# Routing the first two batches in one block and starting the experts at step 13 instead of step 15

## The chip, the core and the metric

The kernel runs on one core of a Trainium2 chip. The metric is the device time of one execution in microseconds (us). The engines of the core work side by side, each through its own instruction queue in order: TensorE (PE, matrix products), VectorE (DVE), ScalarE (ACT), GpSimd (POOL), and SyncE (SP), which here only issues transfers. A transfer issued by POOL with a list of row numbers (an indirect DMA) scatters rows to places in memory.

## The reference, cut to what matters

The input is `x`, 8 batches of 2496 x 256. A two-dimensional Fourier transform is taken of each batch and its real part gives 19968 tokens of 256 features. Each token goes to one of 8 experts (two matrices with a ReLU between them), and its result is scaled by two gate values.

```python
X = np.fft.fft(np.fft.fft(x, axis=1), axis=2).real      # (8, 2496, 256) -> 19968 tokens
logits = X @ w_gate
e_idx = np.argmax(logits, axis=1)
gate_w = softmax(logits)[arange, e_idx]
eom = sigmoid(X @ w_output_gate)
for e in range(8):
    mask = e_idx == e
    out[mask] = gate_w[mask, None] * eom[mask, e, None] * (relu(X[mask] @ w1[e]) @ w2[e])
```

## The kernel before

**Fourier part.** A batch is cut into five chunks along the sequence; chunk m (0 to 39) belongs to batch m // 5. A chunk is loaded (`load_x`, L302), folded by `fold1` (L413, L416, L417, mostly on POOL; L416 and L417 exist from batch 3 on, `LB`) and `fold2` (L429 to L443, mostly DVE), its energy is summed on ACT (L451), and `dstage` (L482 to L486, PE) with `devac` (L494 on ACT, L495 on DVE) transforms the features. Then come five steps of a batch: step n belongs to batch b = n // 5 and has the place i = n % 5. Each is one `sstage` (L521, PE) with `sevac` (L536 to L556, DVE and ACT), which leaves rows of tokens in on-chip memory. During the steps of batch b the loop `steps()` also folds chunks of the next batch or two (`AHEAD` says up to which chunk, place by place), takes the next batch's energy (at place 1) and runs its `dstage` (places 2 to 4).

**Routing.** `gating(b)` starts at the first step of batch b + 1. It finds each token's expert and its row in the scratch memory `scr` (L564 to L647, DVE and ACT, with two small matmuls L597 and L598), and issues 20 scatters (L653, POOL) that write the rows. It is a generator in phases: a `yield "C"` ends a phase, and the loop lets it go on one phase per step. After scatters 4, 9 and 14 (`SPL`) it stops too, so the 20 scatters are spread over four steps with folds of later chunks between them on POOL's queue.

**Tables and experts.** `table_a(i)` lists blocks of tokens for the experts; the first table (`NAS[0]` = 12 slots of 256 tokens) covers the batches 0 and 1 (`BAS`). It ends with `slot_scales` (L712 to L717), which needs the weight scales `wsc`. Those come from the energies of all 16 weight matrices: each is loaded whole (`wload`, L363, two buffers `wt`) and squared on ACT (`wsquare`, L367), at a pace set in `steps()`, and `wscales` (L371 to L378) ends it. A slot of the experts loads its tokens transposed (`load_x_`, L1075, and their gate values L1076), has its weights loaded (`load_w`, L1089) and split into two 16-bit parts (`conv`, L1095 on ACT and L1096 on DVE), runs `mm1` (L1115) and `mm2` (L1135), and scatters the result (L1143, POOL).

**What sets the order.** Up to the end of the routing the queues of SP and POOL follow the order of the program text (`PH1`); the order on PE, ACT and DVE is worked out at build time by a simulated schedule and is then fixed. Steps 0 to `FSTART` = 15 are run before the experts begin. After that `background()` hands out the remaining steps between pieces of the expert slots, at rates worked out from `work`. `load_x` keeps five chunk buffers in the pool `px` and two more in `pw`, the pool on the right side that also holds `wt`; when `pw` is closed, its space goes to the experts' pool `fr` (raw weights, split weights, tokens).

Of the kernel before, what the change touches and what calls it, by code (L numbers as in the profile page):

```python
# [17 lines left out]
NB, S, D, E, F = 8, 2496, 256, 8, 1024  # L18
# [47 lines left out]
FSTART = 5 * BA + MARGIN  # L66

W0, NW = 2, 2

AHEAD = (5, 6, 7, 8, 9), (4, 5, 6, 7, 8)  # L70
# [160 lines left out]
def fft_moe_kernel(ctx: ExitStack, tc: tile.TileContext, xl, wg, w1, w2, tde, tdo, gt, ts0, tsm, tsr, tsq, cst, tid, out):  # L231
# [44 lines left out]
    if True:  # L276
# [16 lines left out]
        def load_x(n=NB * KC):  # L293

            while n and len(xq) < NB * KC:
                q = pw if held[pw] < NX2 and len(xq) < FSTART + 8 else px
                if held[q] == (NX2 if q is pw else NX):
                    break
                held[q] += 1
                b, c = divmod(len(xq), KC)  # L300
                t = q.tile([128, 8, HN], F32, name="xt", tag="xt", bufs=NX2 if q is pw else NX)
                nc.sync.dma_start(t, xl[b, c])  # L302
                xts[b, c] = t
                xq.append(q)
                n -= 1
# [75 lines left out]
        gens = []  # L381

# [36 lines left out]
        def fold2(b, c):  # L419
# [24 lines left out]
            for k in done:  # L444
                xts.pop((b, k))
                held[xq[b * KC + k]] -= 1
                load_x()
                if b == 0:
                    continue
                sq = pf.tile([128, 4, 128], mybir.dt.bfloat16, name="sq", tag="sq", bufs=1)  # L450
                nc.scalar.activation(sq[:, :, 0:KW[k]], f[k].rearrange("p a b n -> p (a b) n")[:, :, 0:KW[k]], AF.Square,  # L451
                                     scale=1.0 if h else 1.5, accum_out=st[b]["en"][:, k:k + 1])
# [105 lines left out]
        def gating(b):  # L558
# [98 lines left out]
            for j in range(20):  # L657
                if b < NB - 1:
                    scatter(j)
                    if j in SPL:  # L660
                        yield "C"
                else:
                    deferred.append(lambda j=j: scatter(j))
# [66 lines left out]
        def table_a(i):  # L730
# [54 lines left out]
            yield  # L785
            yield from slot_scales(ea, n, i)
# [145 lines left out]
        def start():  # L932
# [19 lines left out]
            for c in range(KC):  # L952
                if c > 1:
                    dstage(0, c)
                devac(0, c)

        def steps():
            wk = 0
            fc = KC
            for n in range(5 * NB):  # L960
                b, i = divmod(n, 5)
                if i == 0 and b > 0:
                    add_gen(gating(b - 1))
                smalls.clear()
                ds_ = ((), (), (0, 1), (2, 3), (4,))[i] if b + 1 < NB else ()
# [8 lines left out]
                while fc <= min(KC * (b + 1) + AHEAD[b >= BA][i], KC + 3 * n + 2):  # L974
# [14 lines left out]
                if i == 1 and b + 1 < NB:  # L989
                    energy(b + 1)  # L990
                    energy_sum(b + 1)
                    scale(b + 1)
                weave(piece("A"))
                while wk <= 2 * E and wk < (n - W0 + 1) * (2 * E + 1) / (FSTART - W0):
# [6 lines left out]
                if n == W0 - 1:  # L1001
                    for k in range(NW):
                        wload(k)
# [11 lines left out]
    if True:  # L1015
# [132 lines left out]
        def experts():  # L1148
            chained(load_x_, 0)
# [3 lines left out]
            chained(load_x_, 1)  # L1153
            for h in range(2):
                conv(0, 0, h)
            yield "i"
# [73 lines left out]
    with tc.manual_schedule(engines=PH1):  # L1230
        start()
        steps_ = steps()
        for m in steps_:
            if m == ("step", FSTART):
                break
        rp.close()
        fx.append(pl(ctx, name="fr", bufs=2, side="right"))
# [6 lines left out]
        for _ in table_a(0):  # L1244
            pass
        add_raw(fx[0])
        add_wbuf(fx[0])
# [3 lines left out]
        work = [5 * (b - a) + 45 * C_TAB for a, b in zip(BAS, BAS[1:])] + [5 * (NB - BAS[-1]) - MARGIN + 28 * C_SCAT + 50 * C_TAB + 3.5]  # L1251
        rates = [w / (9.0 * (e - s_)) for w, s_, e in zip(work, [0] + ends, ends)]
        acc, slot = 0.0, 0
        fg = experts()
# [39 lines left out]
```

## Time and profile before

| What | us |
| --- | --- |
| median of 3 runs | 1174.66 |
| lowest and highest of them | 1174.36 and 2767.52 |
| the profiled execution, its own time | 1159.36 |
| its span, first to last instruction | 1157.5 |
| VectorE busy | 833.0 (72%) |
| ScalarE busy | 731.6 (63%) |
| GpSimd busy | 498.6 (43%) |

A row of a timeline gives start, duration, engine, line, operation, the tiles written and read, the number of instructions and, in brackets, how long the engine was idle before it and what ended that. A row of stretches gives a window, its length, the busy time of each engine with its instructions in brackets, the clock granted to TensorE as a share of full speed, the share of time that the DMA engines were busy, and GB/s. A row of waits gives who waited for whom: us in total, times, longest. A row of groups gives busy us, mean ns of one, and idle time before them.

### The profile page before, as it was taken

The numbers are of one execution on the slowest core, as the hardware profiler recorded it, in microseconds if no ns is written. First come the engines' busy times: TensorE is split into PE (matmuls) and PEld (weight loads), VectorE is DVE, ScalarE is ACT, GpSimd is POOL, SyncE is SP. The second block draws the span as 40 slices with busy tenths as digits, with TensorE's granted clock in tenths as the row PEclk, the third lists the DMA queues.
The fourth block names the chain that finished last, engine by engine and source line by source line (L and its number), as shares of the span: only waits on it lengthen the run. The fifth ranks groups of instructions, "written<-read, shape, count | busy, mean of one in ns | idle before, by whom it ended". The sixth has DMA issues, their size and how long they took to land.

```text
span 1157.5 us, 28573 instructions
## 1 busy us (share of the span) xinstructions
PE 1052.7 (91%) x10060; PEld 934.4 (81%) x10060; DVE 833.0 (72%) x1535; ACT 731.6 (63%) x1216; POOL 498.6 (43%) x430
## 2 busy tenths in 40 slices
PE   3877469989999999998999999999999989999998
PEld 3666458878788887887878888889989979998887
DVE  7876797878988747568445454588777867787684
ACT  2598657666666654553445454587777767777684
POOL 5418873786577444462564122223222322322231
PEclk9998779999999999999999999999999999999999
DMA  7778554755547545464767524557457464655651
GB/s 285 300 260 346 214 161 137 222 164 149 168 144 183 138 131 151 137 166 143 186 182 177 142 57 122 154 159 196 128 170 201 125 166 113 175 166 147 183 130 30
DMA packets 158213, 194.09 MB, mean 168 GB/s; under 512 B 117885, under 2 KB 118527, under 8 KB 156020
## 3 DMA queue, kind: packets, MB, share of 16 engines
q1 hardware_dynamic: 142100, 149.68, 46.6%
q0 software_dynamic: 15824, 42.14, 10.9%
q8 instruction: 79, 1.29, 0.5%
q14 instruction: 66, 0.54, 0.2%
q10 hardware_dynamic: 144, 0.44, 0.1%
HBM read 193.47 MB, written 43.46 MB: 205 GB/s over the span
## 4 chain that ended last, share of the span: by engine, by line
PE 63%; DVE 11%; issue 8%; POOL 6%; ACT 5%; DMA 3%; SPq 2%; another core or an unknown queue 0%; POOLq 0%; DVEq 0%; ACTq 0%
PE hp L1115 30%; PE yp L1135 29%; PE psb_t L521 3%; POOL scr L653 2%; POOL out_dram L1143 2%; DVE w1b L1096 1%; DVE rt L549 1%; DMA raw1b<-in_w_dram 1%; DVE hl L1120 1%; POOL xt L413 1%; SPq L1057 1%; ACT wt L367 1%; DVE w0b L1096 1%; DVE xt L432 1%; ACT w1b L1095 1%
## 5 line engine op out<-in xcount | busy, mean ns | idle before, releaser
L1115 PE MATMUL hp<-xr,w0b 128*128 128x256 f16 (+2 forms) x4224 | 482.8, 264 | 20.9 <-DVE hl L1120 13.7
L1135 PE MATMUL yp<-w1b,hh 128*128 128x256 f16 x2608 | 450.4, 273 | 6.7 <-issue 3.6
L1143 POOL DMA_INDIRECT out_dram<-y,xf x163 | 214.7, 1317 | 554.1 <-ACT y L1142 520.2
L1115 PEld LDWEIGHTS <-w0b 128*128 128x128 f16 x4224 | 384.6, 98 | 70.4 <-issue 15.4
L1135 PE MATMUL yp<-w1b,hl 128*128 128x256 f16 (+3 forms) x1304 | 356.0, 273 | 2.0 <-issue 2.0
L1135 PEld LDWEIGHTS <-hh 128*128 128x128 f16 x2608 | 251.9, 98 | 40.3 <-issue 11.9
L1119 ACT ACTIVATE hh<-hp 128x512 f16<-128x512 f32 (+4 forms) x352 | 194.0, 554 | 131.6 <-PE hp L1115 112.9
L1120 DVE SCALAR_TENSOR_TENSOR hl<-hp,hh 128x512 f16<-128x512 f32 (+4 forms) x352 | 222.0, 637 | 68.2 <-ACT hh L1119 56.9
L1096 DVE SCALAR_TENSOR_TENSOR w1b<-raw1b,ssc,w1b 128x1024 f16<-128x1024 f32 x144 | 186.3, 1294 | 111.7 <-ACT w1b L1095 90.3
L1096 DVE SCALAR_TENSOR_TENSOR w0b<-raw0b,ssc,w0b 128x1024 f16<-128x1024 f32 x144 | 190.2, 1324 | 69.6 <-ACT w0b L1095 51.7
L653 POOL DMA_INDIRECT scr<-rows,desti x160 | 178.6, 1116 | 73.3 <-issue 43.8
L1095 ACT ACTIVATE w0b<-raw0b,ssc 128x1024 f16<-128x1024 f32 x144 | 164.6, 1146 | 64.6 <-PE hp L1115 28.6
L1095 ACT ACTIVATE w1b<-raw1b,ssc 128x1024 f16<-128x1024 f32 x144 | 165.2, 1148 | 55.0 <-PE yp L1135 25.0
L1135 PEld LDWEIGHTS <-hl 128*128 128x128 f16 (+3 forms) x1304 | 127.9, 98 | 19.0 <-issue 4.2
L1142 ACT ACTIVATE y<-yp,ysc 128x256 f32<-128x256 f32 (+1 forms) x163 | 68.9, 470 | 43.4 <-PE yp L1135 34.2
L413 POOL TENSOR_TENSOR xt<-xt 128x500 f32<-128x500 f32 (+1 forms) x35 | 47.0, 1346 | 21.8 <-DMA xt<-in_xl_dram 19.5
L482 PE MATMUL psb_t<-tdet,ft 128*125 128x290 f32 (+1 forms) x120 | 36.2, 458 | 16.5 <-DVE alo L495 12.2
L482 PEld LDWEIGHTS psb_t<-tdet,ft 128*125 128x125 f32 (+1 forms) x120 | 24.7, 213 | 25.1 <-issue 13.5
L521 PE MATMUL psb_t<-ahi,tstq 125*128 125x145 f16 (+1 forms) x384 | 41.4, 227 | 3.3 <-DVE rt L539 2.0
L521 PEld LDWEIGHTS <-tstq 125*128 125x128 f16 (+1 forms) x576 | 38.6, 97 | 5.4 <-issue 4.6
L551 ACT CAST rows<-rt 128x516 f16<-128x516 f32 x40 | 25.0, 625 | 21.7 <-DVE rt L549 11.3
L484 PE MATMUL psb_t<-tdet,ft 128*125 128x145 f32 (+1 forms) x100 | 22.9, 313 | 16.8 <-DVE alo L495 9.4
(214 smaller groups left out, 916.4 us busy)
## 6 DMA issues: line engine op xcount, KB each, us to landing
raw0b<-in_w_dram SPq DMA_DIRECT2D x144, 512.0 KB
raw1b<-in_w_dram SPq DMA_DIRECT2D x144, 512.0 KB
xt<-in_xl_dram SPq DMA_DIRECT2D x40, 512.0 KB
wt<-in_w_dram SPq DMA_DIRECT2D x16, 1024.0 KB
out_dram<-y,xf POOLq DMA_INDIRECT x163
scr<-rows,desti POOLq DMA_INDIRECT x160
xr<-scr SPq DMA_TRANSPOSE x88
xf<-scr SPq DMA_DIRECT2D x75, 2.0 KB
```

Of the source, the lines that this page charges most:

```text
L413: eng.tensor_tensor(x0, x0, x1, op=ALU.add)
L482: nc.tensor.matmul(o[:, 0:290], ft[:, k, par, W], tdab[:, k], start=(k == 0), stop=(k == 1))
L521: nc.tensor.matmul(ps[:, k, c0:c0 + 145], tab[hl][t][K], a[K, kc, par, c0:c0 + 145], start=(n == 0), stop=(n == len(terms) - 1))
L653: free_order("scr", batch=b, inst=nc.gpsimd.indirect_dma_start(out=scr[:, :], out_offset=bass.IndirectOffsetOnAxis(ap=desti[:, j:j + 1], a ...
L1095: nc.scalar.activation(w[:, 0], r, AF.Copy, scale=sc)
L1096: nc.vector.scalar_tensor_tensor(w[:, 1], r, sc, w[:, 0], op0=ALU.mult, op1=ALU.subtract)
L1115: nc.tensor.matmul(ps[:, k, T], w1v[:, hl, kc, (f % 4) * 128:(f % 4 + 1) * 128], a["x"][:, x, T], start=(m == 0), stop=(m == 5))
L1119: nc.scalar.activation(hh[:, G, T], ps[:, :, T], AF.Relu)
L1120: nc.vector.scalar_tensor_tensor(hl[:, G, T], ps[:, :, T], 0.0, hh[:, G, T], op0=ALU.max, op1=ALU.subtract)
L1135: nc.tensor.matmul(a["yp"][0:M, u], a[k, h][:, f, u * 128:u * 128 + M], w2v[:, hl, f], start=(g == 0 and f == 0 and m == 0), stop=(h == 1 ...
L1142: nc.scalar.activation(a["y"][0:M, u], a["yp"][0:M, u], AF.Copy, scale=ys[0:M, u:u + 1])
L1143: free_order("out", nc.gpsimd.indirect_dma_start(out=out[:, :], out_offset=bass.IndirectOffsetOnAxis(ap=a["f"].bitcast(I32)[0:M, u, 1:2], ...
```

## The change

Batches 0 and 1 (b < `BA` = 2) are routed without stops between the scatters. At step 10 the whole of `gating(1)` with its 20 scatters, and the first table up to its scales, stand ahead of all else of that step, and from there chunk loads are held (`hold`) until the experts' first tokens are loaded. The folds of the fourth batch (chunks 15 to 19) move behind those scatters; its energy goes to place 3 and all five of its `dstage` to place 4; from the fifth batch on the folds are two chunks later, the energy is at place 2, `dstage` at places 3 and 4. The weight squares begin at step 0 and end at step 11 (before: 2 and 14). After step 12 the first table's scales are worked out, `pw` is closed, and the first expert's weights are loaded and split; after step 13 the rest of the experts begins. The pool `pw` takes chunks below 16 only (before: 23).

```diff
-FSTART = 5 * BA + MARGIN
-W0, NW = 2, 2
-AHEAD = (5, 6, 7, 8, 9), (4, 5, 6, 7, 8)
+MARGIN0 = 3
+FSTART = 5 * BA + MARGIN0
+WEND, NW = FSTART - 1, 2
+AHEAD = {0: (5, 6, 7, 8, 9), BA - 1: (5, 5, 5, 5, 5), BA: (0, 1, 3, 5, 6)}
+AHEAD_ = (2, 4, 5, 5, 6)
+ESTEP = 1, 3, 2
+DSTEP = ((), (), (0, 1), (2, 3), (4,)), ((), (), (), (), (0, 1, 2, 3, 4)), ((), (), (), (0, 1, 2), (3, 4))
...
-                q = pw if held[pw] < NX2 and len(xq) < FSTART + 8 else px
+                q = pw if held[pw] < NX2 and len(xq) < FSTART + 3 else px
...
-                load_x()
+                if not hold:
+                    load_x()
...
-                    if j in SPL:
+                    if j in SPL and b >= BA:
                         yield "C"
...
             yield
+            yield "scales"
             yield from slot_scales(ea, n, i)
...
                 devac(0, c)
+            for k in range(NW):
+                wload(k)
...
+                late = int(b >= BA) + int(b > BA)
                 if i == 0 and b > 0:
                     add_gen(gating(b - 1))
+                    if b == BA:
+                        hold.append(1)
+                        for ph in "CACC":
+                            weave(piece(ph))
+                        first.append(table_a(0))
+                        while next(first[0]) != "scales":
+                            pass
                 smalls.clear()
-                ds_ = ((), (), (0, 1), (2, 3), (4,))[i] if b + 1 < NB else ()
+                ds_ = DSTEP[late][i] if b + 1 < NB else ()
...
-                while fc <= min(KC * (b + 1) + AHEAD[b >= BA][i], KC + 3 * n + 2):
+                while fc <= min(KC * (b + 1) + AHEAD.get(b, AHEAD_)[i], KC + 3 * n + 2):
...
-                if i == 1 and b + 1 < NB:
+                if i == ESTEP[late] and b + 1 < NB:
...
-                while wk <= 2 * E and wk < (n - W0 + 1) * (2 * E + 1) / (FSTART - W0):
+                while wk <= 2 * E and wk < (n + 1) * (2 * E + 1) / WEND:
...
-                if n == W0 - 1:
-                    for k in range(NW):
-                        wload(k)
...
         def experts():
-            chained(load_x_, 0)
             for m in range(2):
                 for h in range(2):
                     chained(load_w, 0, m, h)
-            chained(load_x_, 1)
             for h in range(2):
                 conv(0, 0, h)
+            yield "w"
+            chained(load_x_, 0)
+            hold.clear()
+            chained(load_x_, 1)
             yield "i"
...
         for m in steps_:
+            if m == ("step", WEND):
+                for _ in first[0]:
+                    pass
+                rp.close()
+                fx.append(pl(ctx, name="fr", bufs=2, side="right"))
+                add_raw(fx[0])
+                add_wbuf(fx[0])
+                fg = experts()
+                next(fg)
             if m == ("step", FSTART):
                 break
-        rp.close()
-        fx.append(pl(ctx, name="fr", bufs=2, side="right"))
...
-        for _ in table_a(0):
-            pass
-        add_raw(fx[0])
-        add_wbuf(fx[0])
+        next(fg)
+        load_x()
...
-        work = [5 * (b - a) + 45 * C_TAB for a, b in zip(BAS, BAS[1:])] + [5 * (NB - BAS[-1]) - MARGIN + 28 * C_SCAT + 50 * C_TAB + 3.5]
+        work = [5 * (b - a) + (MARGIN - MARGIN0) * (i == 0) + 45 * C_TAB for i, (a, b) in enumerate(zip(BAS, BAS[1:]))] + [5 * (NB - BAS[-1]) - MARGIN + 28 * C_SCAT + 50 * C_TAB + 3.5]
...
-        fg = experts()
```

More of the change, by code (lines that the diff above doesn't have):

```diff
@@ L381, in fft_moe_kernel @@
         gens = []
+        first, hold = [], []
         def piece(phase):
```

## The prediction

> **What bounds the kernel now.** I read the page first, then a table of stretches.
>
> ```profile
> PE 1052.7 (91%) x10060; PEld 934.4 (81%) x10060; DVE 833.0 (72%) x1535; ACT 731.6 (63%) x1216; POOL 498.6 (43%) x430
> PE   3877469989999999998999999999999989999998
> PEclk9998779999999999999999999999999999999999
> ```
>
> PE is the bound from the seventh slice (some 175 us) on. What can be won lies ahead of that. The stretches from 100 us on are cut where the granted clock changes; the columns are window, length, busy time of PE, weight loads, DVE, ACT and POOL, the clock, and the DMA's share and rate.
>
> ```profile
> 100.00:102.40 2.40, 1.59 (x12) 1.47 (x12) 2.40 (x9) 1.25 (x5) 1.87 (x2) 1.00 0.77 316
> 102.40:109.20 6.80, 5.84 (x36) 5.49 (x36) 6.77 (x23) 6.80 (x14) 5.80 (x4) 0.50 0.63 210
> 109.20:116.10 6.90, 3.21 (x46) 3.02 (x43) 2.73 (x17) 6.71 (x15) 5.59 (x6) 0.99 1.01 399
> 116.10:126.30 10.20, 4.48 (x19) 4.51 (x20) 8.89 (x27) 2.06 (x6) 7.83 (x9) 0.50 0.52 209
> 126.30:139.90 13.60, 8.70 (x115) 8.21 (x113) 8.15 (x14) 11.49 (x22) 11.77 (x12) 1.00 0.77 259
> 139.90:150.20 10.30, 4.15 (x29) 4.04 (x30) 10.27 (x33) 6.20 (x15) 8.68 (x10) 0.50 0.35 117
> 150.20:157.00 6.80, 2.89 (x24) 2.51 (x22) 6.77 (x40) 2.62 (x7) 5.57 (x6) 1.00 0.21 76
> 157.00:167.30 10.30, 4.98 (x39) 4.90 (x38) 9.96 (x22) 4.88 (x9) 9.07 (x10) 0.50 0.58 152
> 167.30:176.00 8.70, 8.70 (x100) 8.38 (x99) 5.03 (x8) 7.25 (x13) 2.23 (x2) 1.00 1.00 243
> ...
> 176.00:600.00 424.00, 393.83 (x3793) 349.13 (x3791) 307.81 (x683) 244.86 (x439) 240.23 (x211) 0.99 0.57 160
> ```
>
> Counting a microsecond at clock 0.50 as half, PE did 1.59 + 2.92 + 3.21 + 2.24 + 8.70 + 2.08 + 2.89 + 2.49 + 8.70 = 34.8 us of full-speed work in these 76 us. So 41.2 us of them are lost. That, and not the moment at which the experts begin, is what the change can shrink: all work that PE does while it waits for the experts' first tokens would have to be done later anyway. What holds the experts back stands on POOL, then on the chain of waits and the timelines of DVE, ACT and PE.
>
> ```profile
> L653 POOL DMA_INDIRECT scr<-rows,desti x40 | 43.3, 1083 | 38.5 <-ACT qs L537 26.3 <-issue 10.5 <-ACT rows L649 0.3
> L413 POOL TENSOR_TENSOR xt<-xt 128x500 f32<-128x500 f32 (+1 forms) x8 | 10.1, 1267 | 0.1
> L416 POOL TENSOR_TENSOR xt<-xt 128x250 f32<-128x250 f32 (+1 forms) x7 | 5.9, 836 | 0.6
> L417 POOL TENSOR_TENSOR xt<-xt 128x250 f32<-128x250 f32 (+1 forms) x7 | 5.2, 742 | 0.0
> 80.69 1.14 POOL L653 DMA_INDIRECT scr<-rows,desti  x1 [26.30 <-ACT qs L537]
> 121.11 1.00 POOL L653 DMA_INDIRECT scr<-rows,desti  x1 [1.34 <-issue]
> 122.41 1.24 POOL L653 DMA_INDIRECT scr<-rows,desti  x1 [0.30 <-issue]
> ...
> 155.44 2.49 DMA scr<-rows,desti
> 157.98 1.35 SPq L1075
> 164.02 0.21 DVE L1139 TENSOR_SCALAR ysc<-xf,ssc 128x2 f32<-128x2 f32 x1
> 164.58 1.15 ACT L1095 ACTIVATE w0b<-raw0b,ssc 128x1024 f16<-128x1024 f32 x1 [0.68 <-DMA raw0b<-in_w_dram]
> 170.03 0.60 PE L1115 MATMUL hp<-xr,w0b 128*128 128x256 f16 x4
> ```
>
> The first four rows group POOL's work from 80 to 156.5 us. Batch 0's scatters begin at 80.69 and batch 1's at 121.11; the last is issued at 155.44 and lands 2.49 later; SP then sends the token transfer, behind it the weights, and the first expert matmul runs at 170.03. Between the scatters stand seven chunks of folds, 1.27 + 0.84 + 0.74 = 2.85 us each, some 20 us in all.
>
> **The change part by part.**
>
> *Scatters in one go.* A scatter costs 1.083 us and the 0.30 of issue behind it, 1.38. Batch 0's twenty then end at 80.7 + 27.7 = 108.4. Batch 1's can start then, if its gating is through.
>
> ```profile
> L521 PE MATMUL psb_t<-ahi,tstq x96: 223/227/230, 55.8 to 93.6; 125*128 125x145 f16 x64, 128*128 128x145 f16 x32
> 68.02 0.33 DVE L564 TENSOR_TENSOR lg<-qs 128x160 f32<-128x160 f32 x1 [0.15 <-ACT qs L547]
> 79.54 0.75 DVE L647 SCALAR_TENSOR_TENSOR rows<-r_se,p_x,r_num 128x4 f32<-128x4 f32 x5
> 101.59 0.32 DVE L564 TENSOR_TENSOR lg<-qs 128x160 f32<-128x160 f32 x1
> 120.12 0.75 DVE L647 SCALAR_TENSOR_TENSOR rows<-r_se,p_x,r_num 128x4 f32<-128x4 f32 x5
> DVE ft L429 <- POOL xt L417: 8.4, 4, 4.6
> ```
>
> The gating takes 12.3 us in batch 0 (68.02 to 80.3) and 19.3 in batch 1. There DVE waited for folds that stood on POOL between scatters, 8.4 us from 80 to 176 us and once 4.6 of it within that gating; these waits go with the folds. The last matmul of step 9 starts at 93.6 (first row), so the gating could begin at some 95.3, and before it began at 101.6, behind a square on ACT and such a fold. I take 98 and 12.3 us: ready at 110.3. The twenty scatters end at 138.0, the last is issued at 136.6 and lands at 139.1. SP needs 1.35 us to issue the token transfer. When the tokens land isn't shown; it is between 0 and 4.7 us behind that issue (159.3 to the reader of the gate values, sent after them, at 164.02). I take 2.2. Experts begin at **142.6**. Early end: gating from 95.3, ready ahead of POOL's 108.4; last issue at 134.7, landing 137.2, tokens with the issue alone at 138.6. Late end: gating as before, ready at 120.9, scatters to 148.6, tokens at 155.7.
>
> *Weights ahead.* From the landing (157.9) to 170.0 the 12 us went into loading and splitting the first weights. Loaded after step 12 they are off this path, and the transfers that SP issues ahead of the tokens' (four of 512 KB) wait for no scatter. One cover is thin: `fr` takes over the space of `pw`, and chunk 15 sits in `pw` until chunk 16 is folded, which POOL does after the last scatter: 138.0 + 2.85, four DVE operations (some 1.6 us), then a split on ACT and DVE of 1.15 + 1.28 gives 144.9, 2.3 us past the tokens, if the half that is needed first lies there. I take nothing for it and keep 2.3.
>
> *What PE has done by then.* After 100 us only steps 12 to 14 are left for it: the fourth batch's `dstage` waits for folds behind the scatters.
>
> ```profile
> 126.90:129.30 2.40, 2.39 (x36) 2.27 (x35) 1.00 0.42 123
> ```
>
> This row is the matmuls of one step of 36. Steps 12, 13 and 14 have 60, 36 and 36, so 132 x 2.39 / 36 = 8.8 us. Lost until the experts: 42.6 - 8.8 = 33.8, against 41.2. That is **7.4 us won** (early end 11.4, late end -5.7).
>
> *What is given back.* The experts begin on an idle PE. The half-clock stretches above are 6.8 to 10.3 us long, the experts of before began inside a full one; up to 5.1 us are lost, none if the stretch has just ended; I take 2.5. Then steps 15 to 17 join the mixed stage, which lost 424.0 - 393.8 = 30.2 us over 22 steps, 1.4 a step: 0 to 4.1, I take 2.0, since one stage of waits need not grow with its steps.
>
> *Weight squares earlier, and the held loads.*
>
> ```profile
> 0.00:100.00 100.00, 18.04 (x18) 0.93 0.79 297
> 25.00:50.00 25.00, 17.43 (x143) 14.26 (x144) 22.48 (x44) 12.89 (x32) 13.69 (x13) 0.82 1.00 383
> 50.00:100.00 50.00, 38.95 (x370) 32.34 (x368) 37.30 (x99) 43.97 (x88) 19.36 (x20) 0.97 0.68 258
> ```
>
> The first row is the squares alone: nine before 100 us (18 rows, two for each, 2.0 us). The new pace puts fifteen by step 9, so 12 us more on ACT, which has 12.1 + 6.0 idle from 25 to 100 us. The cover is the first of these, while the DMA is full at 383 GB/s, into which two more MB fall. Between 0 and 12 us; I take 0 beyond the 2.7 that the gating starts after its early end, since most fit. The held chunk loads cost nothing while chunks 15 to 20 are there for 6 x 2.85 us of folds; SP issues the next right behind the first two token transfers.
>
> *Energy, `dstage` and later folds* change the order and no amount of work; DVE and POOL have 116 and 184 us idle in the 424 of the mixed stage. Zero; what it costs if this cover is gone is a rival below.
>
> The sum: 7.4 - 2.5 - 2.0 = 2.9 us. On the profiled execution 1159.36 - 2.9 = 1156.5; the runs' median lies 15.3 above that execution, so 1174.66 - 2.9 = **1171.8**.
>
> **A row and a rule.** DVE's split of a weight half and a scatter met once:
>
> ```profile
> 166.44 1.28 DVE L1096 SCALAR_TENSOR_TENSOR w0b<-raw0b,ssc,w0b 128x1024 f16<-128x1024 f32 x1
> 166.53 2.03 POOL L653 DMA_INDIRECT scr<-rows,desti  x1 [0.30 <-issue]
> ```
>
> The scatter took 2.03 instead of 1.08. Four splits beside batch 1's scatters would add up to 4 x 0.95 = 3.8 us to the path that sets the start: a loss of 0.9 us in place of the gain, 1175.6. The Trainium skill, page "SBUF — State Buffer", section "SBUF: two separate sides", states such a lock: a DVE operation with two inputs in SBUF and a GpSimd operation exclude each other for a whole instruction. By that rule every such split holds a scatter. The trace agrees in this pair.
>
> **The rivals.**
> 1. *ACT becomes the bound of steps 0 to 9.* For: 44.0 of 50 us busy from 50 to 100. Against: the idle 12.1 before. If six of the twelve us land on the path, the start is 6 later: 1177.8.
> 2. *The clean case.* Without fold waits and with squares in idle time the gating is ready ahead of POOL: 11.4 won, 1 to 2.5 given back: 1164 to 1166.
> 3. *Splits hold scatters*, as above: 1175.6.
> 4. *The split doesn't run beside the scatters.* The squares or chunk 15 hold the space and 12 us stay between landing and start: 139.1 + 12.1 = 151.2, so 41.2 - 42.4 - 4.5 = -5.7: 1180.4.
> 5. *Slower, by one mechanism: the Fourier steps fall behind and the first table's 12 slots run out.* Steps without experts beside them lose what 12 to 17 lost, 41.2 / 6 = 6.9 us each. It decides from four such steps on: 27.6 - 2.9 gives 1199.4. For: the fourth batch is folded behind all scatters of batch 1 instead of between them. Against: 12 slots are long, and POOL is idle for 184 us of the mixed stage.
>
> **How the numbers follow.** Forecast (a small gain, 1168 to 1174) 0.40, rival 1 0.16, rival 2 0.19, rival 3 0.08, rival 4 0.11, rival 5 0.06. The time is the forecast's, 1171.8. The range runs from rival 2 with the clean end's 11.4 whole (1163) to rival 4 with the thin cover's 2.3 and a little more beside it (1184). Two per cent (23.5 us) is about what a measurement of this kernel can tell from no change: all cases but rival 5 stay within it, and a tail of rival 2 goes beyond: faster 0.02, same 0.92, slower 0.06.
>
> **What would show it.** Right: twenty scatters of L653 without L413 between them, the last near 137; L1095 and L1096 on the first weights ahead of the first L1115, which runs near 143; no DVE wait for POOL's folds of 4 us; idle in the mixed stage near 30 us. Wrong: the first L653 well after 81 (rival 1), the first L1115 waiting for a split (rivals 3 and 4), gaps of PE near the end of the twelfth slot (rival 5).

## The result, and the profile after

The changed kernel takes 1210.24 us (median of 4 runs, 1201.2 to 1213.43) beside 1174.51 us before: a ratio of 1.0323, 95% interval 1.0287 to 1.0359. It is slower by 3.2%; 1171.8 us was predicted. Ratios here and below are those of the fast runs on record; the two medians alone give 1.0304. The profiled execution took 1213.43 us, with a span of 1211.6.

First two lines from the page of the changed kernel (busy time, and PE's row of the 40 slices), then stretches of it: window, length, PE's busy time and matmuls, granted clock, DMA share and rate.

```profile
PE 1062.4 (88%) x10060; PEld 936.7 (77%) x10060; DVE 850.6 (70%) x1535; ACT 731.9 (60%) x1216; POOL 499.4 (41%) x430
PE   4985039898989898988978999999999999999998
```

```profile
100.00:125.00 25.00, 14.89 (x162) 0.68 0.46 162
125.00:150.00 25.00, 0.61 (x2) 0.52 0.74 260
150.00:175.00 25.00, 4.21 (x26) 0.52 0.19 48
176.00:600.00 424.00, 382.96 (x3676) 0.97 0.54 149
```

The hole, PE's idle time ahead of the experts, has not shrunk. From 125 to 175 us PE works 4.8 us, at half clock. The first expert product was to run at 142.6; the timelines of POOL, ACT, SP and PE show where it went (start, duration, engine, line, and in brackets the idle time ahead with what ended it):

```profile
81.54 1.14 POOL L661 DMA_INDIRECT scr<-rows,desti  x1 [22.29 <-ACT rows L563]
106.23 0.98 POOL L661 DMA_INDIRECT scr<-rows,desti  x1 [0.30 <-issue]
125.66 0.99 POOL L661 DMA_INDIRECT scr<-rows,desti  x1 [18.45 <-issue]
150.61 0.98 POOL L661 DMA_INDIRECT scr<-rows,desti  x1 [0.30 <-issue]
157.52 0.62 ACT L459 ACTIVATE sq<-ft 128x500 bf16<-128x500 f32 x1 [10.76 <-DVE ft L448]
159.58 2.17 ACT L1111 ACTIVATE w0b<-raw0b,ssc 128x1024 f16<-128x1024 f32 x2
163.65 3.12 SPq L1105 DMA_DIRECT2D raw0b<-in_w_dram  x2
167.57 1.34 SPq L1091 DMA_TRANSPOSE xr<-scr  x1
170.78 1.44 PE L1131 MATMUL hp<-xr,w0b 128*128 128x256 f16 x6 [29.73 <-DMA xr<-scr]
```

There are two delays. Batch 0's twenty scatters run in one go, 81.5 to 107.2, as predicted; then POOL stands idle for 18.45 us until batch 1's gating is through, and batch 1's scatters run from 125.66 to 151.59 instead of 110.3 to 138. And between their end and the first product lie another 19 us: the split of the first weights (L1111) waits on ACT behind a square of chunk 15, which waits for the fold of chunk 16 behind the scatters (chunk 15 itself is still folded on POOL ahead of them; 16 to 19 stand behind); SP's transfer of the tokens (L1091) stands behind the *next* expert's weights (L1105), which wait for that split.

Why the gating was late is seen on PE. These rows are PE's groups from 85 to 112 us, with the idle time ahead of them in the last column:

```profile
L529 PE MATMUL psb_t<-ahi,tstq 125*128 125x145 f16 (+1 forms) x48 | 7.1, 250 | 6.7 <-issue 6.7
L529 PE MATMUL psb_t<-alo,tstq 125*128 125x145 f16 (+1 forms) x24 | 5.4, 243 | 7.7 <-issue 7.7
```

In "issue" PE waits for nothing that the trace shows. After the first few, step 9's matmuls came in ones, twos and threes, every 0.7 us or more, up to 110.5, while the scatters ran; the kernel before did a step of 36 in 2.39 us.

### The profile page after: what moved, and what is told of

Its sections match the earlier page's. It is cut to its first block, busy times and chain, and to the rows that moved or that the text cites. A ratio compares the mean times of both kernels' runs of the same rounds, so it can differ in the third digit from the quotient of the medians.

```text
span 1211.6 us, 28574 instructions
## 1 busy us (share of the span) xinstructions
PE 1062.4 (88%) x10060; PEld 936.7 (77%) x10060; DVE 850.6 (70%) x1535; ACT 731.9 (60%) x1216; POOL 499.4 (41%) x430
## 4 chain that ended last, share of the span: by engine, by line
PE 64%; DVE 11%; issue 9%; ACT 5%; POOL 4%; another core or an unknown queue 3%; DMA 2%; SPq 1%; POOLq 0%; DVEq 0%; ACTq 0%
PE hp L1131 29%; PE yp L1151 27%; PE psb_t L529 5%; POOL scr L661 2%; PE psb_t L490 1%; DVE w1b L1112 1%; DVE hl L1136 1%; DVE w0b L1112 1%; POOL out_dram L1159 1%; ACT w1b L1111 1%; DVE ft L436 1%; PE psb_t L494 1%; DVE xt L439 1%; ACT wt L373 1%
## 5 line engine op out<-in xcount | busy, mean ns | idle before, releaser
L1131 PE MATMUL hp<-xr,w0b 128*128 128x256 f16 (+2 forms) x4224 | 488.5, 265 | 66.9 <-DMA xr<-scr 29.7
L661 POOL DMA_INDIRECT scr<-rows,desti x160 | 175.0, 1094 | 88.7 <-issue 62.9
L1111 ACT ACTIVATE w0b<-raw0b,ssc 128x1024 f16<-128x1024 f32 x144 | 164.3, 1145 | 75.1 <-PE hp L1131 44.5
L1111 ACT ACTIVATE w1b<-raw1b,ssc 128x1024 f16<-128x1024 f32 x144 | 165.0, 1147 | 64.1 <-PE yp L1151 31.5
L1158 ACT ACTIVATE y<-yp,ysc 128x256 f32<-128x256 f32 (+1 forms) x163 | 69.0, 470 | 36.7 <-PE yp L1151 31.8
L490 PE MATMUL psb_t<-tdet,ft 128*125 128x290 f32 (+1 forms) x120 | 40.6, 499 | 15.8 <-DVE alo L503 7.9
L459 ACT ACTIVATE sq<-ft 128x500 bf16<-128x500 f32 (+1 forms) x35 | 21.8, 623 | 47.0 <-DVE ft L448 40.1
L503 DVE SCALAR_TENSOR_TENSOR alo<-psb_t,p_x,ahi 125x580 f16<-125x580 f32 (+1 forms) x40 | 32.1, 814 | 21.8 <-ACT ahi L502 20.4
L490 PEld LDWEIGHTS psb_t<-tdet,ft 128*125 128x125 f32 (+1 forms) x120 | 27.1, 234 | 25.9 <-issue 10.6
```

Source lines behind the costliest of these rows:

```text
L490: nc.tensor.matmul(o[:, 0:290], ft[:, k, par, W], tdab[:, k], start=(k == 0), stop=(k == 1))
L661: free_order("scr", batch=b, inst=nc.gpsimd.indirect_dma_start(out=scr[:, :], out_offset=bass.IndirectOffsetOnAxis(ap=desti[:, j:j + 1], a ...
L1111: nc.scalar.activation(w[:, 0], r, AF.Copy, scale=sc)
L1131: nc.tensor.matmul(ps[:, k, T], w1v[:, hl, kc, (f % 4) * 128:(f % 4 + 1) * 128], a["x"][:, x, T], start=(m == 0), stop=(m == 5))
L1158: nc.scalar.activation(a["y"][0:M, u], a["yp"][0:M, u], AF.Copy, scale=ys[0:M, u:u + 1])
```

## The experiments

Three theories. *Theory 1:* the order of the queues behind the scatters (fold, square, split, next weights, tokens) delays the start. *Theory 2:* a long run of scatters starves PE's issue and with it the gating. *Theory 3:* the Fourier work that was put off costs more beside the experts than the 2.0 us predicted. The runs fell on five chips, each group on one; a ratio is always to the kernel before on the same chip, whose time was 1133 to 1135 on chips 1 and 11 and 1159 to 1161 on chips 7, 9 and 12. The gaps column sums PE's issue gaps over 0.3 us between 60 and 130 us.

| run | chip | time, us | ratio (95% interval) | first scatter of batch 1 | first product | gaps |
|---|---|---|---|---|---|---|
| e1_pause | 11 | 1162.60 | 1.0248 (1.0219–1.0277) | 121.4 | 166.4 | 0 |
| e2_tokens | 11 | 1150.45 | 1.0141 (1.0113–1.0169) | 107.3 | 142.5 | 0 |
| e3_fold16 | 11 | 1148.36 | 1.0108 (1.0070–1.0146) | 112.3 | 145.3 | 0 |
| e5_all | 11 | 1153.61 | 1.0173 (1.0145–1.0201) | 125.4 | 157.1 | 0 |
| b0_before | 1 | 1133.67 | 0.9991 (0.9967–1.0016) | 122.9 | 171.3 | 0 |
| a0_after | 1 | 1147.79 | 1.0104 (1.0073–1.0136) | 107.1 | 152.6 | 0 |
| e4_both | 1 | 1144.08 | 1.0078 (1.0051–1.0105) | 113.1 | 146.7 | 0 |
| e6_late | 1 | 1143.03 | 1.0077 (1.0052–1.0102) | 111.3 | 144.6 | 0 |
| e7_foldall | 7 | 1187.86 | 1.0231 (1.0189–1.0273) | 127.5 | 172.5 | 13.0 |
| e8_start15 | 7 | 1198.93 | 1.0346 (1.0302–1.0390) | 126.0 | 176.7 | 13.8 |
| a1_after | 7 | 1192.32 | 1.0297 (1.0246–1.0349) | 123.8 | 169.3 | 13.7 |
| a2_after | 9 | 1193.88 | 1.0296 (1.0252–1.0340) | 123.6 | 168.9 | 14.0 |
| p2_pause6 | 9 | 1187.81 | 1.0249 (1.0205–1.0293) | 114.2 | 160.6 | 4.3 |

**Pauses between batch 0's scatters (e1_pause).**

```diff
                     scatter(j)
+                    if j in SPL and b == 0:
+                        for _ in range(12):
+                            nc.gpsimd.memset(ptile, 0.0)
```

> The changed kernel with 12 small memsets on POOL (about 0.3 us each, 3.7 us in all) behind scatters 4, 9 and 14 of batch 0, so that no more than five scatters of batch 0 run on end; everything else as in the changed kernel. Theory 2 (a long run of scatters starves PE's issue, so that step 9's 36 matmuls take 20 us instead of 2.3 and batch 1's gating starts at 114.6): PE's issue gaps between 80 and 112 us fall from 14.5 us to under 3, step 9 ends by 95, batch 1's gating is ready by 110, and its first scatter goes out when POOL is through with the pauses, near 118 to 119 instead of 125.7; time 1201 to 1205 (6 to 9 us less than the changed kernel). Theory 1 alone (what counts is the order of the queues behind the scatters): step 9 stays slow and batch 1's first scatter stays at 125 or later; time within 3 us of 1210.

On this chip there was nothing to mend: none of the four kernels of the group shows an issue gap there, pauses or not. The pauses only moved batch 1's scatters 14 us back. It answers nothing on theory 2, but prices a late start: against e2_tokens the first product is 23.9 us later and the time 12.2 us longer.

**Tokens ahead of the next weights (e2_tokens).**

```diff
-                conv(0, 0, h)
+                conv(0, 0, h, False)
...
             chained(load_x_, 1)
+            for h in range(2):
+                chained(load_w, after_new[0], 0, h)
```

> The changed kernel with SP's order changed at the start of the experts: the two loads of tokens are asked for ahead of the second expert's weights, which wait for the splits. Theory 1: the transposing loads of xr go out when the last scatter of batch 1 has landed, near 154, instead of 167.6; the first product (L1131 of the changed kernel) then waits for the split of the first weights, not for xr, and starts at 163 to 166 instead of 170.8; time 1204 to 1207. If the tokens' own landing is what is late (the rival within theory 1: the loads are slow, not late), xr lands at 170 all the same and the time stays within 2 us of 1210. Batch 1's scatters stay at 125.7 to 151.6 under either.

**Folds ahead of batch 1's scatters (e3_fold16).**

```diff
-AHEAD = {0: (5, 6, 7, 8, 9), BA - 1: (5, 5, 5, 5, 5), BA: (0, 1, 3, 5, 6)}
+AHEAD = {0: (5, 6, 7, 8, 9), BA - 1: (5, 5, 5, 5, 7), BA: (0, 1, 3, 5, 6)}
```

> The changed kernel with chunks 15 and 16 and 17 folded two chunks sooner (the last step of batch 1 folds up to 7 chunks ahead instead of 5), so that no fold stands between batch 1's scatters and the first split. Theory 1: ACT's and DVE's splits of the first weights run beside batch 1's scatters, ending near 150 instead of 170.1; the tokens are asked for as soon as the scatters have landed, near 154; the first product starts at 157 to 160 instead of 170.8; time 1196 to 1201. Rival (the splits are slow by themselves beside scatters, or wait for the raw weights or the scales): the splits end after 160 and the time stays within 4 us of 1210. Theory 2 expects nothing to change before 125 us.

**All three (e5_all).**

> All three edits together: pauses between batch 0's scatters, tokens ahead of the second expert's weights, chunks 16 and 17 folded before batch 1's scatters. Theories 1 and 2 together: batch 1's scatters from near 118 to 144, first product at 149 to 153, time 1186 to 1195. If the two were all that the prediction missed, the time would be near 1180 (prediction 1171.8 plus 7 for the pauses); what is left above that is theory 3, the later Fourier steps costing more in the mixed stage than the 4.5 us predicted.

The first two starts came out well ahead of what was expected (142.5 and 145.3), because the chip had no gaps and batch 1's scatters began at 107 and 112 without help. With the pauses, e5_all put its scatters at 125.4 and started at 157.1, 4 us later than the latest expected. The time did not follow the start: with the first product at 142.5, where the prediction had it, e2_tokens still takes 1.4% more than the kernel before. Nor is its ratio smaller than that of a0_after below (1.0104, on another chip), which starts 10.1 us later. So the start is not all that was missed.

**The two kernels again, on another chip (b0_before, a0_after).**

> The kernel before, unchanged, once more with a trace, on the chip of this group, so that the others can be set against it on one chip (the group before ran it in 1133 us, the first measurement in 1175). PE idle in all near 99 us as in the first trace if the chip alone sets the difference by its speed; fewer gaps of PE's own issue (16 gaps over 0.3 us behind runs of five scatters in the first trace) if those are what the first chip did worse.

> The changed kernel, unchanged, once more with a trace, on the same chip as the others of this group. Theory 2 (scatters on end starve PE's issue wherever it runs): step 9 stretched from 91 to 110 us again, batch 1's scatters from 125 us, ratio to before 1.032. Rival (the starving belongs to the first chip): no issue gaps at 91 to 110, batch 1's scatters from 107, first product (L1131) at 150 to 155, held by the splits and the queue of SP (theory 1), and a ratio of 1.015 to 1.025.

The rival holds in the trace: on chip 1 the same changed kernel shows no gap, batch 1's scatters follow batch 0's at 107.1, and the first product is at 152.6. The ratio, 1.0104, is below the 1.015 to 1.025 that it expected. The second delay is there undiminished:

```profile
132.25 0.98 POOL L661 DMA_INDIRECT scr<-rows,desti  x1 [0.30 <-issue]
133.25 1.26 POOL L420 TENSOR_TENSOR xt<-xt 128x500 f32<-128x500 f32 x1
136.00 1.44 DVE L436 TENSOR_TENSOR ft<-xt 128x250 f32<-128x250 f32 x1 [6.18 <-POOL xt L424]
139.16 0.62 ACT L459 ACTIVATE sq<-ft 128x500 bf16<-128x500 f32 x1 [8.18 <-DVE ft L448]
141.22 2.17 ACT L1111 ACTIVATE w0b<-raw0b,ssc 128x1024 f16<-128x1024 f32 x2
145.30 3.12 SPq L1105 DMA_DIRECT2D raw0b<-in_w_dram  x2
149.22 1.34 SPq L1091 DMA_TRANSPOSE xr<-scr  x1
152.56 3.69 PE L1131 MATMUL hp<-xr,w0b 128*128 128x256 f16 x18 [27.34 <-DMA xr<-scr]
```

Read downwards, this is the chain of theory 1, one engine handing to the next: scatters end on POOL, fold on POOL, fold on DVE, square on ACT, split on ACT, next weights on SP, tokens on SP. The tokens are asked for 16 us after the last scatter (133.23 to 149.22), and the first product comes 19.3 us after it. Of these, POOL's fold takes 2.7 us, DVE's four operations 4.5 (to 140.5), the rest of ACT's squares 0.7, the splits of both halves on ACT and DVE 7.1 (to 148.3); 0.9 more until the tokens are asked for, and 3.3 until they are used.

**Both queue edits (e4_both), and the later batches' schedule as before (e6_late).**

> The changed kernel with the tokens ahead of the second expert's weights and with chunks 16 and 17 folded before batch 1's scatters. Theory 1: splits done before the last scatter lands and tokens asked for at once, so on a chip without issue gaps the first product stands at 142 to 144, within 3 us of either edit alone (142.5 and 145.3), and the time within 4 us of theirs, a ratio of 1.008 to 1.014. Rival (each edit wins back its own part): first product before 139, ratio under 1.005.

In the trace of e4_both the splits run beside the scatters, and the tokens are asked for 1.5 us behind the last one (141.76). Three scatters that meet splits on DVE (130.34 to 136.96) take 1.6 to 1.9 us instead of 0.98, one of them shown here, and the run of twenty takes 28.7 us, where it took 26.1 in a0_after:

```profile
128.63 1.15 ACT L1111 ACTIVATE w0b<-raw0b,ssc 128x1024 f16<-128x1024 f32 x1 [0.94 <-DVE ssc L725]
133.30 2.18 ACT L1111 ACTIVATE w1b<-raw1b,ssc 128x1024 f16<-128x1024 f32 x2
134.70 1.91 POOL L661 DMA_INDIRECT scr<-rows,desti  x1 [0.30 <-issue]
140.78 0.98 POOL L661 DMA_INDIRECT scr<-rows,desti  x1 [0.30 <-issue]
143.25 1.34 SPq L1091 DMA_TRANSPOSE xr<-scr  x1
146.67 4.08 PE L1132 MATMUL hp<-xr,w0b 128*128 128x256 f16 x24 [19.50 <-DMA xr<-scr]
```

The chain of theory 1 is shown and undone. The start comes 5.9 us sooner than in a0_after (the two folds set ahead put the scatters themselves back by 6), though 2.7 us later than expected at the latest; the time is 3.7 us less, and the two intervals overlap.

The next edit, e6_late, goes on top of both:

```diff
-AHEAD_ = (2, 4, 5, 5, 6)
+AHEAD_ = (4, 5, 6, 7, 8)
-ESTEP = 1, 3, 2
+ESTEP = 1, 3, 1
```

(and the fourth tuple of the second stage's steps likewise)

> The kernel with both edits, and for the fifth batch on the folds, the energy's step and the steps of the second stage as in the kernel before (4, 5, 6, 7, 8 chunks ahead, energy at step 1, second stage at steps 2, 3 and 4). Theory 3 (later folds and energies cost the mixed stage time): 4 to 12 us less than with both edits alone, a ratio near 1.00. Rival (the loss is the half clock and the idle 100 to 143 us, not the later schedule): within 2 us of both edits.

Same time as e4_both: the later schedule from the fifth batch on costs nothing that shows.

These are the stretches of the kernel before, the changed kernel and both edits, on chip 1, same columns as above:

```profile
0.00:100.00 100.00, 69.30 (x552) 0.93 0.79 292
100.00:150.00 50.00, 26.72 (x243) 0.68 0.67 245
150.00:175.00 25.00, 17.54 (x138) 0.68 0.58 147
175.00:400.00 225.00, 209.08 (x2094) 1.00 0.62 166
400.00:700.00 300.00, 300.00 (x2848) 1.00 0.62 156
```

```profile
0.00:100.00 100.00, 73.71 (x642) 0.95 0.82 301
100.00:150.00 50.00, 1.79 (x15) 0.55 0.57 198
150.00:175.00 25.00, 20.98 (x182) 0.88 0.59 169
175.00:400.00 225.00, 206.95 (x2054) 0.98 0.59 164
400.00:700.00 300.00, 298.02 (x2846) 1.00 0.62 152
```

```profile
0.00:100.00 100.00, 71.51 (x608) 0.95 0.81 298
100.00:150.00 50.00, 7.11 (x69) 0.56 0.69 225
150.00:175.00 25.00, 22.42 (x221) 1.00 0.67 190
175.00:400.00 225.00, 207.06 (x2057) 0.97 0.58 160
400.00:700.00 300.00, 298.28 (x2840) 1.00 0.62 153
```

Busy time times clock is PE's work in full-speed microseconds. Up to 175 us it is 64.4 + 18.2 + 11.9 = 94.5 before, 70.0 + 1.0 + 18.5 = 89.5 changed, 67.9 + 4.0 + 22.4 = 94.3 with both edits. From 175 to 400 it is 209.1, 202.8 and 200.8; from 400 to 700 it is 300.0, 298.0 and 298.3. So the changed kernel is behind by 5.0 + 6.3 + 2.0 = 13.3 us (its span by 13.7), and both edits by 0.2 + 8.3 + 1.7 = 10.2 (span 9.9). What is left with a good start is lost in the mixed stage.

**More work moved ahead (e7_foldall, e8_start15), and the changed kernel beside them (a1_after).**

```diff
-AHEAD = {0: (5, 6, 7, 8, 9), BA - 1: (5, 5, 5, 5, 7), BA: (0, 1, 3, 5, 6)}
+AHEAD = {0: (5, 6, 7, 8, 9), BA - 1: (5, 6, 7, 8, 10), BA: (0, 1, 3, 5, 6)}
-ESTEP = 1, 3, 2
+ESTEP = 1, 1, 2
```

(and the third tuple of the second stage's steps as the first); e8_start15 has `MARGIN0 = 5` besides.

> The kernel with both edits (tokens first; folds ahead of batch 1's scatters), now with all five chunks of the fourth batch and the first of the fifth folded before batch 1's scatters (5, 6, 7, 8, 10 ahead), its energy at step 11 and its second stage at steps 12 to 14, beside the scatters; experts still after step 12. By the two chunks that cost POOL 5.8 us before batch 1's scatters in the kernel with both edits, three more put the first of them at 121 to 123 and the first product at 150 to 154, 8 us later than there. Theory 3 (the mixed stage of the first table is bound by what DVE and PE have to do in it, so that work moved ahead counts and the start alone doesn't): PE works in the hole at 105 to 150, and the time is 0 to 6 us under both edits alone, a ratio of 1.002 to 1.008. Rival (every us of the start counts in full): 5 to 9 us over both edits, a ratio of 1.012 to 1.016.

> The same, and the experts begin after step 14 as in the kernel before, two steps later than in the changed kernel, so that two more Fourier steps run in the hole and leave the first table's slots. Theory 3: PE idle in 100 to 150 falls by another 5 us, the first product stays at 150 to 156 (the scatters set it), fewer waits for DVE's hl and no dips of the granted clock at 200 to 340; time 3 to 8 us under the one with five chunks, a ratio of 0.993 to 1.003. Rival (start counts in full): the two steps hold the first product to 158 or later, ratio 1.012 or more.

> The changed kernel once more beside them. If it falls on a chip on which PE's issue starves behind scatters: step 9 from 91 to 110 us, ratio 1.025 to 1.035; otherwise as in the last group, ratio 1.008 to 1.013, first product near 152.

This chip has the gaps, in all three. The expectations, made for a chip without them, were missed. Set against a1_after, e7_foldall starts 3.2 us later and takes 4.5 us less, with intervals that overlap: a hint that work done in the hole is worth something, not a proof. e8_start15, with two more steps ahead, takes 11.1 us more than e7_foldall, where theory 3 expected it to gain.

Neither start was set by the scatters, as the expectations had it. The last square of the weights ended at 160.2 us in e7_foldall and at 166.2 in e8_start15, against 138.7 in a1_after. In e8_start15 the squares also run to step 13 instead of 11, since `WEND` follows `MARGIN0`, and the first split waited for the scales that they give:

```profile
170.47 1.15 ACT L1111 ACTIVATE w0b<-raw0b,ssc 128x1024 f16<-128x1024 f32 x1 [1.46 <-DVE ssc L725]
```

The Fourier steps moved into the hole met batch 1's scatters there: in e8_start15 PE has 7.7 us more of issue gaps, from 145 to 155 us. So this run moves three things at once and decides nothing on theory 3.

**Shorter pauses on a chip with gaps (a2_after, p2_pause6).** The edit is that of e1_pause with 6 memsets for 12.

> The changed kernel beside the next three, on their chip. On a chip on which PE's issue starves: issue gaps of 13 to 15 us at 90 to 112, batch 1's scatters from 124 to 126, ratio 1.025 to 1.035; on one on which it doesn't, scatters from 107 and 1.008 to 1.013.

> The changed kernel with 6 memsets on POOL (1.9 us) behind scatters 4, 9 and 14 of batch 0. On a chip on which PE's issue starves, theory 2: the gaps at 90 to 112 fall from 14 us to under 4, batch 1's gating is ready by 110 and its scatters start at 113 to 116 instead of 124 to 126, the first product 8 to 11 us sooner, the time 5 to 11 us under the changed kernel. If it is the number of scatters, not their lying end to end, that starves PE: no change of the gaps, the same start, the time within 3 us. On a chip without the gaps: 5.7 us later start, 4 to 6 us more time.

Theory 2 holds for the gaps. First POOL's first scatter of batch 1 in the timeline of a2_after, with its idle time; then the same scatter in p2_pause6; then the first of PE's groups from 85 to 112 us in p2_pause6 (three others there have issue gaps, of 1.3, 1.0 and 0.5 us; a2_after has two such groups, with 10.6 and 3.5).

```profile
123.58 0.99 POOL L661 DMA_INDIRECT scr<-rows,desti  x1 [16.43 <-issue]
```

```profile
114.19 1.00 POOL L662 DMA_INDIRECT scr<-rows,desti  x1 [0.31 <-ACT wt L374]
```

```profile
L530 PE MATMUL psb_t<-ahi,tstq 125*128 125x145 f16 (+1 forms) x72 | 9.2, 248 | 1.7 <-issue 1.7
```

As many scatters, broken by 1.9 us after every fifth, leave 4.3 us of gaps for 14.0, POOL has no idle time between the batches, and the first product stands 8.3 us sooner. The medians differ by 6.1 us, as expected, though the intervals overlap.

**Extra work for DVE (x1_after_dve, x0_before_dve, then x1_after_dveb, x0_before_dveb, a3_after).** Four instructions behind each fold of batches 3 and 4, in both kernels; the first pair set a tile to zero, the second copied the tile just written:

```diff
             eng.tensor_sub(ft[:, :, 1, W], v[:, :, 0, W], v[:, :, 1, W])
+            if b in (3, 4):
+                for _ in range(4):
+                    nc.vector.tensor_copy(dtile[:, :, W], ft[:, :, 1, W])
```

> The changed kernel with four memsets on DVE (some 0.3 to 0.4 us each) behind each chunk's fold of batches 3 and 4, 40 in all, 12 to 16 us of DVE time in the first table's mixed stage. Theory 3 (DVE sets that stage): 9 to 16 us more than the changed kernel, 70% or more of what is added. Rival (PE sets it, DVE's idle time takes the work): 0 to 5 us more.

> The same 40 memsets in the kernel before, where some of batch 3's folds lie ahead of the experts and DVE is busy 85% of 175 to 400. Theory 3: 3 to 8 us more than the kernel before, clearly less than the changed kernel pays. Rival (both stages are bound alike): the same as the changed kernel pays.

> The changed kernel on the chip of the next two: ratio 1.008 to 1.013 where PE's issue doesn't starve, 1.025 to 1.035 where it does.

> The changed kernel with four copies on DVE (some 0.4 us each) of the tile that the fold has just written, behind each chunk's fold of batches 3 and 4, 40 in all, 16 us of DVE time, nearly all between 160 and 400 us. Theory 3 (DVE sets that stage): 11 to 18 us more than the changed kernel, 70% or more of what is added. Rival (PE sets it, DVE's idle time takes the work): 0 to 6 us more.

> The same 40 copies in the kernel before. Theory 3: 4 to 10 us more than the kernel before, clearly less than the changed kernel pays. Rival (both stages are bound alike): as much as the changed kernel pays.

The first pair (chip 9: 1199.53 us, 1.0362, 1.0303–1.0421; and 1163.07 us, 1.0042, 1.0017–1.0066) put its work in the wrong place and tells nothing of the stage: in x1_after_dve the memsets, depending on nothing, ran first of all (first and last start at the end of the numbers).

```profile
L440 DVE MEMSET dtile<- x40: 272/272/272, 0.9 to 38.3; 128x256 f32 x40
```

The copies stand behind the folds, first in x1_after_dveb, then in x0_before_dveb:

```profile
L440 DVE COPY dtile<-ft x40: 277/285/1333, 67.2 to 232.7; 128x250 f32<-128x250 f32 x32, 128x256 f32<-128x256 f32 x8
L433 DVE COPY dtile<-ft x40: 277/285/817, 60.0 to 162.9; 128x250 f32<-128x250 f32 x32, 128x256 f32<-128x256 f32 x8
```

But they missed the stage too. In the changed kernel 9.5 us of them lie from 150 to 175 us, nearly all ahead of the first product at 172.1, and only 6.5 from 175 to 400; in the kernel before the last starts at 162.9, so none lies in the mixed stage. On chip 12 the changed kernel goes from 1200.30 (1.0324, 1.0291–1.0357) to 1204.05 us (1.0361, 1.0329–1.0393), 3.8 us more, with a first product 2.6 us later and intervals that overlap. Where 16 us in the stage were to cost 11 to 18, 6.5 us there can't tell theory 3 from its rival. The kernel before goes from 1160.74 to 1166.86 us (1.0035, 1.0012–1.0058) and says nothing of the stage. Whether DVE sets the mixed stage stays open.

No version beat the kernel before.

## Why the prediction was wrong

*What held.* Batch 0's scatters: 80.7 to 108.4 predicted, 81.5 to 107.2 measured. Squares earlier at no cost: on chip 1 the last ends at 124.5, ahead of the scatters' end at 133.2, and in the first measurement at 140.4, ahead of 151.6. Half clock at the start: 2.5 predicted; 20.98 x 0.12 = 2.5 in a0_after from 150 to 175 us. The time that the fourth batch's `dstage` waits behind the scatters, and the price of later folds (0; e6_late).

*"Ready at 110.3" failed on the chip predicted for.* The step took PE's matmuls of step 9 as they stood in the trace before, where scatters come in fives with folds between them. Twenty on end starved PE's issue, the gating began at 114.6 instead of 98, and batch 1's scatters at 125.7. On chips 1 and 11 nothing starved, and the scatters came at the early end of the prediction (107; the gating of a0_after began at 94.9). The trace before had hints: 0.3 us gaps at 96 to 97 us, behind five scatters, and longer ones further on. The ratios, 1.0323 there and 1.0104 on chip 1, lie some 2% apart. The pauses win 8.3 us of start and 6.1 us of time back on such a chip: they show the cause of the late gating, not that of all the 2%, since p2_pause6 still stands at 1.0249. No run there has both the pauses and the edits of e4_both.

*"The transfers that SP issues ahead of the tokens' wait for no scatter" failed on every chip.* It counted the first expert's four loads, but `conv` also chains the next expert's, and these wait for the split. The thin cover was named in its right place (the fold behind the scatters), but taken at nothing. The fold's DVE operations took 4.5 us beside POOL's folds instead of 1.6, and the squares between that fold and the split, on ACT, were left out (0.7). From the scatters' end to the first product the prediction had 4.6 us (138.0 to 142.6); it took 19.3 on chip 1 and 19.2 in the first measurement, 14.7 more. On chip 1 the scatters ended 4.8 us sooner than predicted, so the start is 10 us late (152.6 for 142.6). Rival 4 named this mechanism; that its 151.2 comes so near is luck, as it set out from scatters 6 us later. Whether the split waited for the space that chunk 15 held or only for its turn on ACT isn't told apart. Undoing the chain took 5.9 us off the start and 3.7 off the time.

*"I take 2.0" for the mixed stage was a third of it.* From 175 to 400 us the changed kernel falls 6.3 us behind on chip 1: idle 225.0 - 206.95 = 18.0 against 15.9, and 206.95 x 0.02 = 4.1 us of clock, where the kernel before kept 1.00 throughout. In a0_after the clock is lost after single waits of 2 to 3.4 us, as in these stretches; the same ones of b0_before, whose longest wait from 175 to 400 is 1.9 us, all have 1.00.

```profile
260.00:270.00 10.00, 6.59 (x65) 0.92 0.15 52
270.00:280.00 10.00, 10.00 (x84) 0.91 0.92 269
320.00:330.00 10.00, 6.17 (x72) 0.99 0.75 167
330.00:340.00 10.00, 10.00 (x85) 0.84 0.16 54
```

Each dip follows a wait for `hl` or `y` (3.4 us at 268, 2.3 and 1.5 at 327 and 330); a wait of 2.1 us for `es` at 207 has one of 0.85 beside it. The limit isn't sharp: in the first measurement two waits of 0.7 and 1.0 us at 308 to 310 are followed by a dip too (0.62 and 0.53 in steps of 2 us). The prediction counted a loss per step and no clock. Both kernels have ten waits for `hl` there, 10.2 us in a0_after and 8.7 in b0_before; they are longer, not more. Why stays open: the stage has more Fourier steps per expert product (52 `hl` and 30 `eo` operations on DVE in a0_after, 59 and 24 in b0_before), but the extra DVE work hardly reached it, and the later batches' schedule cost nothing.

*The sum on each kind of chip.* The prediction had PE 7.4 - 2.5 = 4.9 us of work ahead at 175 us, 2.0 of it given back later. On chip 1 PE was 5.0 behind, lost 6.3 from 175 to 400 and 2.0 more to 700: 9.9 + 4.3 + 2.0 = 16.2 us off, which is the 2.9 that were forecast and the 13.3 that were lost. On the chip predicted for, the late start weighs most. From the same windows of the first measurement's two traces PE did 67.57 x 0.93 + 27.76 x 0.73 + 15.77 x 0.79 = 95.6 us of work by 175 us before and 68.65 x 0.89 + 15.50 x 0.60 + 4.21 x 0.52 = 72.6 changed. That is 23.0 behind; 12.3 more are lost from 175 to 400, and 18.5 (taken in steps of 100 us) from 400 to 700, a stretch in which the prediction counted nothing (before, then changed):

```profile
400.00:700.00 300.00, 285.98 (x2650) 0.99 0.54 145
400.00:700.00 300.00, 268.19 (x2499) 0.98 0.56 147
```

The changed kernel's 31.8 us of idle there are 16.9 of issue gaps and 13.2 of waits for `hl` in the main; the kernel before has 11.7 and 1.0. (These two traces lie 54.1 us apart, the medians 35.7. On chip 12 the traces of x0_before_dveb and a3_after lie 34.8 apart, in the same three parts 20.9, 9.9 and 5.0.) No run undoes the last two terms, and their cause stays open.

*The view itself.* The prediction held PE's lost work up to 176 us to be what counts. It is the largest term where PE's issue starves, but not the whole: e4_both has the start nearly as predicted (146.7) and PE's work level with before at 175 us, and still takes 9.4 us more. The 7.4 us were not won there, since the start was 4.1 late, and the half clock of the first products took the rest. Then comes the mixed stage. A late start is dear only in part, as far as pairs tell that differ in more than the start: in the time, e1_pause against e2_tokens shows half of it, a2_after against p2_pause6 three quarters, e5_all against e2_tokens a fifth (3.2 of 14.6 us).

*The rivals.* The first scatter stood at 81.5, so not rival 1. Rival 2's ready gating came true on chips 1 and 11, without its time. Rival 3's stretched scatters could not come in the changed kernel, whose splits ran behind the scatters; in e4_both, where they ran beside them, three scatters took 2.3 us more in all, of the 3.8 that rival 3 counted. With the sides exchanged the stretching is in the changed kernel too: beside POOL's folds the splits of DVE on the first weights took 1.75 and 2.26 us (161.88, 164.41), and 1.27 where POOL left them alone. By the Trainium skill, page "SBUF — State Buffer", section "SBUF: two separate sides", either engine waits for the other's whole instruction; the trace agrees. Rival 5's gaps near the twelfth slot did not come: on chip 1 the 24th result scatter, two to a slot, goes out at 381 us, and no wait of PE from 360 to 430 is over 1.2 us. The profiled execution of the first measurement has 11.9 us of idle from 600 to 700, 7.1 of it behind `hl`, where a1_after, a2_after and a3_after have 1.5, 2.1 and 5.3; that stays unexplained.

## What to carry to other kernels

Before a transfer that many wait for is moved behind other work, write down its whole queue, with everything that helpers chain into it: here the tokens waited for the next weights, these for a split, that for a square, that for a fold behind the very scatters that the change meant to run beside. Interleaving that looks like a delay may be what keeps another engine supplied, so a long run of one instruction should be tried before its neighbours' times are taken over from the trace with the interleaving. Work put off was not moved for nothing here: on chip 1 the stage that took it had single waits of 2 to 3.4 us where the longest had been 1.9, and the clock went with them. And before extra work is taken as a test of a stage, its place in both traces should be looked at: here most of it ran elsewhere.

## What the hardware showed that was not expected

Runs of indirect scatters on POOL can starve PE's issue: 13.0 to 14.4 us of gaps in 20 us, on the chip of the first measurement and on chips 7, 9 and 12, and none over 0.3 us with the same kernel on chip 1, nor on chip 11, where four kernels close to it ran. The gaps begin some 10 us into the run and end some 3 us behind its last scatter. The chips with gaps also run the kernel before slower (1159 to 1175 us against 1133 to 1135), and there it has gaps of its own behind five scatters (12.1 us in all past 130 us in the first trace). What the scatters and PE's instruction supply share isn't shown. From 80 to 115 us the packets of 16 KB in queue q8, which carries instructions, took about 1.1 us each on either kind of chip (one at 0.2% of 16 engines' time in the first measurement, two at 0.4% on chip 1); the trace doesn't say for which engine.
